# Attention probabilities of a fused kernel: both heads of a row tile side by side for all pairs, and six pairs instead of eight transposed in fp32 on TensorE

## The chip, the cores and the metric

The kernel runs on one core of a Trainium2 chip. The metric is the device time of one launch in microseconds (us), lower is better. Below, PE is TensorE (PEld its weight load), DVE is VectorE, ACT is ScalarE, POOL is GpSimd, and SP is the engine whose queue starts nearly all the DMAs.

## The reference

Three stages on a batch of 4, 448 tokens and 768 channels, all in fp32. First a causal attention with 12 heads of 64 channels; then a mixer over tokens and channels ("moe"); then a second mixer with sine and cosine ("moe2").

```python
scores = scale * np.matmul(q, k.transpose(0, 1, 3, 2))
mask = np.triu(np.ones((seq, seq), dtype=bool), k=1)
scores = np.where(mask, -1000000000.0, scores)
scores = scores - np.max(scores, axis=-1, keepdims=True)
attn = np.exp(scores)
attn = attn / (np.sum(attn, axis=-1, keepdims=True) + 1e-09)
return np.matmul(attn, v).astype(np.float32)
...
xt = x.transpose(0, 2, 1)
h = np.maximum(xt @ w_tok1, 0.0) @ w_tok2
u = x + h.transpose(0, 2, 1)
h2 = np.maximum(u @ w_ch1, 0.0) @ w_ch2
return (u + h2).astype(np.float32)
```

The second mixer follows on the result of the first and starts late in the kernel; the change does not touch it.

## The kernel before, in words

The heads are taken in 24 pairs, numbered 0 to 23, six to a batch element. A pair has seven score tiles (`TILES`): one shared tile for the first 64 rows of both heads (row tile 0, 128 columns), then for row tiles 1, 2 and 3 one tile for each head, 192, 320 and 448 columns wide. For a score tile, PE multiplies q with k into a PSUM bank (`ps_sc`, three banks), one DVE operation adds the mask and finds the row minimum of the negated scores while it writes them to SBUF (tile `sb`, line 367), and ACT takes the exponential with the row sum (line 369). The probabilities must then be transposed before PE can multiply them with v.

There are two ways for that. Pairs in `NATPV` (0 to 7) are *native*: PE transposes each 128-column block in fp32 into a PSUM bank (line 376), ACT copies the bank to SBUF (`pt`, line 378), and PE multiplies each block with v in fp32 (line 407), which the trace shows as two instructions for a product. The other pairs, 8 to 23, are *split*: the probabilities of both heads of a row tile stand side by side in one buffer (`both`); ACT makes an fp16 high part and DVE an fp16 low part of them (tile `ph`, lines 387 and 388; two buffers, one for row tiles 0 and 2, one for 1 and 3), one DMA on SP's queue transposes both parts (line 391), and PE makes three fp16 products for a block (lines 416 and 424). A split pair needs its v in two fp16 parts too (`value_squares`, `value_split`: one ACT pass, a small chain over PE, DVE and POOL, one POOL pass, one DVE pass at line 323). Native tiles rotate over three buffers for the probabilities and five for the transposed blocks.

Products with v are made four steps (score tiles) behind the scores for native pairs and five for split ones (`late_steps`). After each second pair comes the token mixing of these two pairs (`tokmix`: 24 short products with `xg`, then transposes and products with `wt2`). When the six pairs of a batch element are done, `split_ready` scales the result into fp16 tiles `ut`, and 72 units of 18 fp16 products with weights (`ch1_unit`, `ch2_unit`) follow, placed between the score tiles from step 53 (in pair 7) on by `UNIT_STEPS`. The weights arrive as float64 words and are rounded and split during the steps 14 to 92, on ACT, POOL and DVE (lines 177, 130, 185, 186, 163, 197), stored to DRAM and loaded again for each batch element.

Every engine works through its instructions in a fixed order that is settled when the kernel is built; score tiles and late steps have a raised priority in it. SP's queue is in order too, so that a DMA that waits for its source holds the loads and stores behind it.

Of the kernel before, what the change touches and what calls it, by code (L numbers as in the profile page):

```python
# [54 lines left out]
def fused(ctx, tc, q, k, v, w_tok1, w_tok2, w_ch1, w_ch2, w_theta, w_tok, w_ch, out):  # L55
# [198 lines left out]
    sb_all = ac.tile([P, BUFS["sb"] * 512], F32, tag="sb", name="sb")  # L254
    sbufs = [sb_all[:, j * 512:(j + 1) * 512] for j in range(BUFS["sb"])]
    for sb in sbufs:
        nc.gpsimd.memset(sb[:, 0:64], 0.0)
    pt_all = ac.tile([P, BUFS["pt"] * 512], F32, tag="pt", name="pt")
    ptfs = [pt_all[:, j * 512:(j + 1) * 512].rearrange("p (n q) -> p n q", q=P) for j in range(BUFS["pt"])]
    blocks = pt_all.bitcast(F16).rearrange("p (n q) -> p n q", q=P)  # L260
    count = [0]
# [135 lines left out]
    def pv(pp, i, h):  # L397
        if pp.ps is None:
            pp.ps = bank("pv", 1)
        reg = 0 if i == 0 else ((i - 1) * 2 + h + 2) * D  # L400
        if pp.native_pv:
            pt = pp.pts[i, h]
            blks = [8] if i == 0 else [6 + h] + [2 * u + h for u in range(i)]
            for u, vt in enumerate(blks):
                n = 2 * D if reg < 7 * D else D
# [6 lines left out]
        pt = pp.pts[i]
        reg = 0 if i == 0 else 2 * i * D
        if i == 0:
            for n, (blk, c) in enumerate(((0, 0), (0, 1), (1, 0))):
# [610 lines left out]
```

## Time and profile before

| | |
|---|---|
| median of 3 runs | 871.08 us (870.21 to 874.33) |
| profiled execution | 871.68 us, span on the core 869.9 us |
| PE busy | 839.3 us, 96% |
| DVE busy | 598.9 us, 69% |
| ACT busy | 531.3 us, 61% |
| POOL busy | 265.6 us, 31% |
| granted TensorE clock, mean | 0.998 |

The span runs from the first to the last instruction; 1.8 us of the device time lie around it. A busy PE here holds instructions that are pipelined, so that two can stand as busy at once, and a short wait can hide behind the end of the one before. What the shares hide is that the kernel has stages with different limits; they are read from windows below.

### The profile page before, as it was taken

To read this page: it belongs to the slowest core of one execution; us is meant where nothing else is said; L and a number is where in the kernel's file an instruction comes from. 1 tells how busy PE (TensorE), PEld (TensorE's weight loads), DVE (VectorE), ACT (ScalarE), POOL (GpSimd) and SP (SyncE) were. 2 spreads that over 40 slices of the span, in tenths; PEclk is the share of its full clock that TensorE was granted. 3 is DMA by queue.
4 is the path that set the end of the run, shared out by engine and by line. 5 is a ranking of instruction groups with operands and counts; after the bars stand their busy time and mean duration, and the time that the engine had idled before them with its cause. 6 is when DMAs were issued, how large, how long until landed. Compare 5 with 4: busy or idle time off the path is not lost.

```text
span 869.9 us, 16014 instructions
## 1 busy us (share of the span) xinstructions
PE 839.3 (96%) x5699; PEld 532.7 (61%) x5699; DVE 598.9 (69%) x1294; ACT 531.3 (61%) x1223; POOL 265.6 (31%) x445
## 2 busy tenths in 40 slices
PE   7999998899899999999999999999999999999997
PEld 6988856565657566576756655565555555555554
DVE  6788787999988556567774367669747548567541
ACT  6798786777767637367653276547647447456441
POOL 4366564547662220413222035331111001101000
PEclk9999999999999999999999999999999999999999
DMA  6866869999999976856475597702613123131012
GB/s 217 258 208 201 269 198 271 261 310 294 289 255 313 280 226 140 233 132 125 141 173 203 186 278 265 227 30 73 197 40 108 40 90 98 40 119 58 25 45 75
DMA packets 121024, 151.99 MB, mean 175 GB/s; under 512 B 76848, under 2 KB 88048, under 8 KB 120944
## 3 DMA queue, kind: packets, MB, share of 16 engines
q1 hardware_dynamic: 120400, 149.95, 59.4%
q0 software_dynamic: 384, 0.79, 0.4%
q8 instruction: 45, 0.74, 0.3%
q10 hardware_dynamic: 160, 0.23, 0.1%
q14 instruction: 35, 0.29, 0.1%
HBM read 110.56 MB, written 22.81 MB: 153 GB/s over the span
## 4 chain that ended last, share of the span: by engine, by line
PE 67%; DMA 10%; DVE 8%; ACT 5%; issue 5%; POOL 5%; SPq 0%; ACTq 0%; POOLq 0%; DVEq 0%
PE ps_mm L232 15%; PE ps_mm L231 15%; PE ps_mm L233 15%; DMA pt<-ph 5%; PE ps_sc L358 3%; PE ps_sc L231 3%; PE ps_sc L232 3%; PE ps_sc L233 3%; PE ps_pv L407 2%; DMA raw_w<-in_w_theta_dram 1%; PE ps_pv L424 1%; ACT junk L124 1%; ACT sb L369 1%; DVE sb L367 1%; PE ps_mm L376 1%
## 5 line engine op out<-in xcount | busy, mean ns | idle before, releaser
L231 PE MATMUL ps_mm<-h,ws 128*128 128x448 f16 x432 | 151.7, 354 | 1.6 <-DVE g L140 1.0
L232 PE MATMUL ps_mm<-h,ws 128*128 128x448 f16 x432 | 152.7, 354 | 0.1
L233 PE MATMUL ps_mm<-h,ws 128*128 128x448 f16 x432 | 152.5, 354 | 0.0
L231 PEld LDWEIGHTS <-ws 128*128 128x128 f16 x720 | 70.5, 98 | 67.2 <-issue 5.3
L233 PEld LDWEIGHTS <-ws 128*128 128x128 f16 x720 | 70.5, 98 | 63.9 <-issue 3.7
L232 PEld LDWEIGHTS <-ws 128*128 128x128 f16 x720 | 70.5, 98 | 62.5 <-issue 5.2
L369 ACT ACTIVATE sb<-sb,mx 128x320 f32<-128x320 f32 (+3 forms) x168 | 89.1, 533 | 25.6 <-DVE mx L367 25.0
L231 PE MATMUL ps_mm<-ut,ws 128*128 128x448 f16 x288 | 101.1, 353 | 1.4 <-DMA rawt<-x2d 1.3
L232 PE MATMUL ps_mm<-ut,ws 128*128 128x448 f16 x288 | 101.5, 353 | 0.8 <-DVE ut L197 0.8
L233 PE MATMUL ps_mm<-ut,ws 128*128 128x448 f16 x288 | 101.6, 353 | 0.0
L367 DVE CUSTOM_DVE_ANT_0 sb<-ps_sc,mask 128x320 f32<-128x320 f32 (+3 forms) x168 | 73.4, 455 | 17.7 <-PE ps_mm L376 11.3
L124 ACT ACTIVATE junk<-acc 128x448 bf16<-128x448 f32 x72 | 41.2, 572 | 59.1 <-DVE acc L912 41.3
L358 PE MATMUL ps_sc<-k_pad,q_raw 128*128 128x192 f32 (+3 forms) x168 | 56.9, 441 | 9.1 <-DMA k_pad<-in_k_dram 4.3
L787 POOL TENSOR_SCALAR tmp<-tmp 128x384 f32<-128x384 f32 x28 | 15.6, 556 | 148.6 <-ACT tmp L786 145.6
L388 DVE SCALAR_TENSOR_TENSOR ph<-sb,ph 128x128 f16<-128x128 f32 (+1 forms) x64 | 46.8, 736 | 19.0 <-ACT ph L160 18.3
L163 POOL TENSOR_SCALAR h<-t 128x448 f16<-128x448 f32 x48 | 35.2, 735 | 75.7 <-ACT t L497 75.2
L497 ACT ACTIVATE t<-ps_mm,c_scale 128x448 f32<-128x448 f32 x48 | 30.0, 625 | 41.3 <-PE ps_mm L233 36.2
L160 ACT ACTIVATE ph<-sb 128x128 f16<-128x128 f32 (+1 forms) x64 | 39.6, 625 | 25.6 <-DMA pt<-ph 25.3
L499 DVE TENSOR_TENSOR h<-t,h 128x448 f16<-128x448 f32 x48 | 32.0, 670 | 27.0 <-POOL h L163 26.9
L130 POOL TENSOR_SCALAR raw<-raw 128x768 f32<-128x768 f32 (+2 forms) x34 | 35.4, 1041 | 41.6 <-ACT wf L177 37.0
L231 PE MATMUL ps_sc<-th,ut 128*128 128x384 f16 x144 | 46.9, 326 | 0.0
L233 PE MATMUL ps_sc<-th,ut 128*128 128x384 f16 x144 | 46.8, 326 | 0.0
(218 smaller groups left out, 2119.4 us busy)
## 6 DMA issues: line engine op xcount, KB each, us to landing
ws<-w_c SPq DMA_DIRECT2D x120, 384.0 KB, 4.6
raw<-in_w_ch_dram SPq DMA_DIRECT2D x30, 768.0 KB, 5.6
w_c<-ws SPq DMA_DIRECT2D x30, 384.0 KB, 4.3
v_raw<-in_v_dram SPq DMA_DIRECT2D x24, 288.0 KB, 4.9
q_raw<-in_q_dram SPq DMA_DIRECT2D x12, 448.0 KB, 4.2
k_raw<-in_k_dram SPq DMA_DIRECT2D x12, 448.0 KB, 5.4
x2d<-acc SPq DMA_DIRECT2D x24, 224.0 KB, 3.8
acc<-x2d SPq DMA_DIRECT2D x24, 224.0 KB, 2.6
```

The lines of the kernel that those rows point to most:

```text
L124: nc.scalar.activation(j[:, 0:src.shape[-1]], src, AF.Square, accum_out=dst)
L130: nc.gpsimd.tensor_scalar(out=dst, in0=a, scalar1=b, scalar2=c, op0=ALU.mult, op1=ALU.mult)
L160: nc.scalar.activation(dst, src, AF.Copy, scale=scale)
L163: e.tensor_scalar(out=dst, in0=src, scalar1=scale, scalar2=0.0, op0=ALU.mult, op1=ALU.add)
L231: nc.tensor.matmul(ps, lhsT=ka(a[:, 0]), rhs=kb(b[:, 0]), start=first, stop=False)
L232: nc.tensor.matmul(ps, lhsT=ka(a[:, 0]), rhs=kb(b[:, 1]), start=False, stop=False)
L233: return nc.tensor.matmul(ps, lhsT=ka(a[:, 1]), rhs=kb(b[:, 0]), start=False, stop=last)
L358: nc.tensor.matmul(ps[:, 0:n], lhsT=lhs, rhs=cut(pp.kh), start=True, stop=pp.kl is None)
L367: pp.first = nc.vector.tensor_tensor_reduce(out=sb, in0=src, in1=msk, op0=ALU.add, op1=ALU.min, scale=-0.125, scalar=3.0e38, accum_out=pp. ...
L369: pp.last = nc.scalar.activation(sb, sb, AF.Exp, bias=pp.mx[:, j:j + 1], scale=-1.0, accum_out=pp.sm[:, 2 + j:3 + j])
L388: nc.vector.scalar_tensor_tensor(out=lo, in0=both, scalar=PSC, in1=hi, op0=ALU.mult, op1=ALU.subtract)
L499: gates[0] = nc.vector.tensor_tensor(out=t[:, 1], in0=f, in1=t[:, 0], op=ALU.subtract)
```

## The change

All pairs now lay the probabilities of both heads of a row tile side by side in `both`, native pairs too. A native row tile is transposed once both heads are there: 128, 384, 640 and 896 columns are 1, 3, 5 and 7 blocks, 16 for a pair, where 1, 2 x 2, 2 x 3 and 2 x 4 were 19 (the middle block now holds 64 columns of each head). Up to four blocks share a PSUM bank and an ACT copy, so that a pair has 6 copies and not 7. The number of fp32 products stays at 19. The three buffers for probabilities become two halves of the same memory, one for row tiles 0 and 2 and one for 1 and 3; the five buffers for transposed blocks become the fixed places that split pairs use. The products of both heads of a row tile are made in the step of the second head. Pairs 6 and 7 leave `NATPV` and become split pairs. The host's layout of k and v follows.

```diff
-BUFS = dict(ut=12, h2=8, acc=12, ws=8, wf=3, raw=3, sb=3, pt=5, t=3, junk=1)
+BUFS = dict(ut=12, h2=8, acc=12, ws=8, wf=3, raw=3, t=3, junk=1)
-NATPV = {0, 1, 2, 3, 4, 5, 6, 7}
+NATPV = {0, 1, 2, 3, 4, 5}
...
-        if pp.native_pv:
-            full = sbufs[count[0] % BUFS["sb"]]
-            sb = full[:, 64:64 + kk]
-        else:
-            both = (sb_all[:, 0:640], sb_all[:, 640:1536])[i % 2][:, 0:P if i == 0 else 2 * kk]
-            sb = both[:, h * kk:(h + 1) * kk]
+        both = (sb_all[:, 0:640], sb_all[:, 640:1536])[i % 2][:, 0:P if i == 0 else 2 * kk]
+        sb = both[:, h * kk:(h + 1) * kk]
...
-        if pp.native_pv:
-            nt = 1 + i
-            c0 = 64 if i == 0 else 0
-            pst = mm_bank()
-            for u in range(nt):
-                nc.tensor.transpose(pst[:, u * P:(u + 1) * P], full[:, c0 + u * P:c0 + (u + 1) * P], ident)
-            pt = ptfs[count[0] % BUFS["pt"]]
-            nc.scalar.activation(pt[:, 0:nt].rearrange("p n q -> p (n q)"), pst[:, 0:nt * P], AF.Copy)
-            pp.pts[i, h] = pt
-            count[0] += 1
-            return
         if i > 0 and h == 0:
             return
         m = both.shape[-1]
+        first = {3: 26, 2: 16, 1: (10, 0)[pp.pr % 2], 0: (8, 6)[pp.pr % 2]}[i]
+        if pp.native_pv:
+            pt = pp.pts[i] = blocks32[:, first // 2:first // 2 + m // P]
+            for u0 in range(0, m // P, 4):
+                pst = mm_bank()
+                nt = min(4, m // P - u0)
+                for u in range(nt):
+                    nc.tensor.transpose(pst[:, u * P:(u + 1) * P], both[:, (u0 + u) * P:(u0 + u + 1) * P], ident)
+                nc.scalar.activation(pt[:, u0:u0 + nt].rearrange("p n q -> p (n q)"), pst[:, 0:nt * P], AF.Copy)
+            return
```

The order moves at three places that matter below. In the rows, line numbers are those of each kernel; line 358 of before is line 349 of the changed kernel, 376 is 368, 407 is 400, 448 is 424, 367 is 354.

**First place.** PE, from the last score tile of pair 4 (448 columns) into pair 5 (its tile of 128 columns); `ident,sb` are transposes, `v_raw,pt` products with v, `xg` token mixing. Before:

```order
L358 MATMUL ps_sc<-k_pad,q_raw 128x448
L376 MATMUL ps_mm<-ident,sb 128x128 x2
L136 LDWEIGHTS ones
L136 MATMUL ps_mm<-tiny,ones 128x1
L376 MATMUL ps_mm<-ident,sb 128x128 x3
L407 MATMUL ps_pv<-v_raw,pt 128x128
L138 LDWEIGHTS ones
L138 MATMUL ps_mm<-sqb,ones 128x1
L358 MATMUL ps_sc<-k_pad,q_raw 128x128
L407 MATMUL ps_pv<-v_raw,pt 128x128 x2
L376 MATMUL ps_mm<-ident,sb 128x128 x3
L358 MATMUL ps_sc<-k_pad,q_raw 128x192
```

The changed kernel, from the same score tile:

```order
L349 MATMUL ps_sc<-k_pad,q_raw 128x448
L349 MATMUL ps_sc<-k_pad,q_raw 128x128
L368 MATMUL ps_mm<-ident,sb 128x128 x5
L400 MATMUL ps_pv<-v_raw,pt 128x128 x5
L349 MATMUL ps_sc<-k_pad,q_raw 128x192
L138 LDWEIGHTS ones
L138 MATMUL ps_mm<-sqb,ones 128x1
L424 MATMUL ps_mm<-xg_686,wt_184 128x256
L400 MATMUL ps_pv<-v_raw,pt 128x128
L424 MATMUL ps_mm<-xg_686,wt_184 128x256
L400 MATMUL ps_pv<-v_raw,pt 128x128 x4
L349 MATMUL ps_sc<-k_pad,q_raw 128x192
```

Before, the six transposes of pair 4's row tile 2 stand in two threes, one on either side of the tile that opens pair 5. Now its five stand together behind that tile. Those of row tile 3 (two fours before, seven now) come behind the token mixing that begins here, some forty rows further on, in both kernels.

**Second place.** PE, from the tile of 128 columns that opens pair 7. Before (the products are those of pair 6, in fp32):

```order
L358 MATMUL ps_sc<-k_pad,q_raw 128x128
L407 MATMUL ps_pv<-v_raw,pt 128x128 x5
L376 MATMUL ps_mm<-ident,sb 128x128 x3
L407 MATMUL ps_pv<-v_raw,pt 128x128 x3
L448 MATMUL ps_mm<-xg_1070,wt_184 128x256 x2
L358 MATMUL ps_sc<-k_pad,q_raw 128x192 x2
L457 MATMUL ps_mm<-ident_128,x_191 128x64
L459 MATMUL ps_mm<-ident,x_191 128x128 x3
L407 MATMUL ps_pv<-v_raw,pt 128x128 x3
L449 MATMUL ps_mm<-xg_1071,wt_184 128x256
L450 MATMUL ps_mm<-xg_1070,wt_184 128x256
L448 MATMUL ps_mm<-xg_1070,wt_184 128x256
```

The changed kernel, a little after the same tile:

```order
L349 MATMUL ps_sc<-k_pad,q_raw 128x192
L400 LDWEIGHTS pt
L400 MATMUL ps_pv<-v_hi,pt 128x128
L400 LDWEIGHTS pt
L400 MATMUL ps_pv<-v_raw,pt 128x128
L400 LDWEIGHTS pt
L400 MATMUL ps_pv<-v_hi,pt 128x128
L424 MATMUL ps_mm<-xg_1037,wt_184 128x256 x2
L400 LDWEIGHTS pt
L400 MATMUL ps_pv<-v_hi,pt 128x64
L400 LDWEIGHTS pt
```

The products of pair 6 are now fp16 products with `v_hi` and `v_raw` that read a block transposed by DMA, no transposes stand here, and the token mixing of pairs 4 and 5 (`xg`) comes behind the first of these products.

**Third place.** DVE, from the mask operation that opens pair 7 (`mask_181` is `mask0`, that of row tile 0). Before:

```order
L367 ISA sb,mx<-ps_sc,mask_181 128x128
L367 ISA mx 128x1
L127 TENSOR_SCALAR g<-g 128x1
L185 SCALAR_TENSOR_TENSOR wf<-wf,raw 128x768
L430 RECIPROCAL sm<-sm 128x7
L186 SCALAR_TENSOR_TENSOR wf<-raw,wf 128x768
L197 SCALAR_TENSOR_TENSOR ws<-wf,s,ws 128x768
L452 SCALAR_TENSOR_TENSOR h_1232<-ps_mm,h_1232 128x256 x2
L367 ISA sb,mx<-ps_sc,mask 128x192
L367 ISA mx 128x1
L467 TENSOR_TENSOR acc<-ps_mm,acc 128x448 x2
```

The changed kernel, from the same operation:

```order
L354 ISA sb,mx<-ps_sc,mask_181 128x128
L354 ISA mx 128x1
L374 SCALAR_TENSOR_TENSOR ph<-sb,ph 128x896
L185 SCALAR_TENSOR_TENSOR wf<-wf,raw 128x768
L354 ISA sb,mx<-ps_sc,mask 128x192
L354 ISA mx 128x1
L354 ISA sb,mx<-ps_sc,mask 128x192
L354 ISA mx 128x1
L197 SCALAR_TENSOR_TENSOR ws<-wf,s,ws 128x768
L374 SCALAR_TENSOR_TENSOR ph<-sb,ph 128x128
L186 SCALAR_TENSOR_TENSOR wf<-raw,wf 128x768
L428 SCALAR_TENSOR_TENSOR h_1229<-ps_mm,h_1229 128x256 x2
```

Between the mask operations of pair 7 there now stand the low parts (`ph`) of row tile 3 of pair 6 and of row tile 0 of pair 7, with the roundings (`wf`, `ws`) still among them.

## Rows read from the trace of the kernel before

**Rows 1.** Page: busy time and share of the span of each engine.

```profile
PE 839.3 (96%) x5699; PEld 532.7 (61%) x5699; DVE 598.9 (69%) x1294; ACT 531.3 (61%) x1223; POOL 265.6 (31%) x445
```

**Rows 2.** Windows: length, busy (count) per engine, PEclk, DMA share, GB/s.

```profile
5.12:79.66 74.54, 73.46 (x511) 63.72 (x511) 59.16 (x157) 61.94 (x176) 37.30 (x56) 1.00 0.74 231
79.66:130.09 50.43, 46.80 (x312) 35.61 (x311) 42.59 (x103) 40.45 (x105) 32.80 (x47) 1.00 0.73 224
113.85:130.09 16.24, 15.90 (x92) 10.07 (x93) 15.39 (x37) 12.69 (x33) 9.36 (x13) 1.00 0.59 152
130.09:148.72 18.63, 15.96 (x136) 12.19 (x135) 15.20 (x36) 10.98 (x30) 8.65 (x13) 1.00 1.07 269
148.72:305.50 156.78, 145.76 (x1200) 95.18 (x1197) 135.62 (x308) 111.18 (x269) 77.18 (x112) 0.99 1.04 284
305.50:869.90 564.40, 556.48 (x3543) 325.14 (x3543) 343.82 (x683) 305.47 (x647) 106.12 (x207) 1.00 0.44 130
```

**Rows 3.** DVE timeline (start, us): the mask operation that opens pairs 6 to 9.

```profile
79.66 0.28 DVE L367 CUSTOM_DVE_ANT_0 sb<-ps_sc,mask 128x128 f32<-128x128 f32 x1
...
91.53 0.28 DVE L367 CUSTOM_DVE_ANT_0 sb<-ps_sc,mask 128x128 f32<-128x128 f32 x1
...
113.85 0.28 DVE L367 CUSTOM_DVE_ANT_0 sb<-ps_sc,mask 128x128 f32<-128x128 f32 x1
...
130.09 0.28 DVE L367 CUSTOM_DVE_ANT_0 sb<-ps_sc,mask 128x128 f32<-128x128 f32 x1
```

**Rows 4.** Waits of DVE from 79 to 131: us in total, times, longest.

```profile
DVE ws L197 <- POOL ws L163: 3.4, 3, 1.8
DVE sb L367 <- PE ps_mm L376: 3.2, 3, 1.9
```

**Rows 5.** PE timeline: start, length, operation, count of merged instructions.

```profile
45.40 1.00 PE L407 MATMUL ps_pv<-v_raw,pt 128*128 128x64 f32 x8
46.24 0.97 PE L358 MATMUL ps_sc<-k_pad,q_raw 128*128 128x448 f32 x2
...
52.10 1.04 PE L376 MATMUL ps_mm<-ident,sb 128*128 128x128 f32 x8
52.97 0.17 PE L136 MATMUL ps_mm<-tiny,ones 128*128 128x1 bf16 x1
...
149.75 0.35 PE L233 MATMUL ps_mm<-ut,ws 128*128 128x448 f16 x1
149.94 0.35 PE L231 MATMUL ps_mm<-ut,ws 128*128 128x448 f16 x1
...
150.54 0.22 PE L424 MATMUL ps_pv<-v_hi,pt 128*128 128x64 f16 x2
150.60 0.19 PE L424 MATMUL ps_pv<-v_raw,pt 128*128 128x64 f16 x1
```

**Rows 6.** Page, costliest groups: busy us, mean ns; idle before, releaser.

```profile
L388 DVE SCALAR_TENSOR_TENSOR ph<-sb,ph 128x128 f16<-128x128 f32 (+1 forms) x64 | 46.8, 736 | 19.0 <-ACT ph L160 18.3
...
L160 ACT ACTIVATE ph<-sb 128x128 f16<-128x128 f32 (+1 forms) x64 | 39.6, 625 | 25.6 <-DMA pt<-ph 25.3
```

**Rows 7.** By tile (pt, then v_raw): duration ns min/median/max; DMA landing.

```profile
L391 SPq DMA_TRANSPOSE pt<-ph x64: 1172/1525/4723, 119.3 to 451.8; - x64
L378 ACT ACTIVATE pt<-ps_mm x56: 256/475/611, 9.6 to 116.2; 128x256 f32<-128x256 f32 x16, 128x384 f32<-128x384 f32 x16, 128x512 f32<-128x512 f32 x16, 128x128 f32<-128x128 f32 x8
...
DMA to landing us min/median/max: 2.3/4.3/9.1
...
L323 DVE SCALAR_TENSOR_TENSOR v_raw<-v_raw,sv,v_hi x16: 861/882/1512, 114.9 to 461.7; 128x576 f16<-128x576 f32 x16
```

**Rows 8.** Chain that ended last: start, us, what.

```profile
129.26 6.33 DMA pt<-ph
...
135.63 6.28 DMA pt<-ph
```

**Rows 9.** Tile sb to 130 us: idle of its engine until the release.

```profile
  PE ps_mm L376: 11.3, 13
```

More of the change, by code (lines that the diff above doesn't have):

```diff
@@ L252, in fused @@
     wt2 = ac.tile([P, 2, 2, S], F32R, tag="wt2", name="wt2")
[L254 to L261, printed above, removed]
+    sb_all = ac.tile([P, 1536], F32, tag="sb", name="sb")
+    pt_all = ac.tile([P, 2560], F32, tag="pt", name="pt")
+    blocks32 = pt_all.rearrange("p (n q) -> p n q", q=P)
+    blocks16 = pt_all.bitcast(F16).rearrange("p (n q) -> p n q", q=P)
     def tok_weights(n):
@@ L399, in pv @@
             pp.ps = bank("pv", 1)
[L400 to L405, printed above, removed]
-                rhs = twice(pp.v[0][:, vt * D:(vt + 1) * D]) if i == 0 else pp.v[0][:, vt * D:vt * D + n]
-                pp.pv = nc.tensor.matmul(pp.ps[:, reg:reg + n], lhsT=pt[:, u], rhs=rhs,
-                                 start=(u == 0), stop=(u == len(blks) - 1))
-            return
@@ L410, in pv @@
         if i > 0 and h == 0:
             return
[L412 to L415, printed above, removed]
-                pp.pv = nc.tensor.matmul(pp.ps[:, 0:2 * D], lhsT=pt[:, blk], rhs=twice(pp.v[c][:, 8 * D:9 * D]),
-                                         start=n == 0, stop=n == 2)
-            return
-        nb = 2 * i + 1
-        for h in range(2):
-            jobs = [(i, 6 + h)] + [(i + 1 + u if h else i - 1 - u, 2 * u + h) for u in range(i)]
-            for n, (blk, vt) in enumerate(jobs):
-                for m, (half, c) in enumerate(((0, 0), (0, 1), (1, 0))):
-                    pp.pv = nc.tensor.matmul(pp.ps[:, reg + h * D:reg + (h + 1) * D], lhsT=pt[:, half * nb + blk],
-                                             rhs=pp.v[c][:, vt * D:(vt + 1) * D], start=n + m == 0, stop=n == i and m == 2)
+        pt, nb = pp.pts[i], 2 * i + 1
@@ new lines, in pv @@
+        parts = ((0, 0),) if pp.native_pv else ((0, 0), (0, 1), (1, 0))
+        for h in range(2 if i > 0 else 1):
+            reg = (2 * i + h) * D
+            n = 2 * D if i == 0 or (pp.native_pv and reg < 7 * D) else D
+            if i == 0:
+                jobs = [(0, 8)]
+            else:
+                jobs = [(i, 6 + h)] + [(i + 1 + u if h else i - 1 - u, 2 * u + h) for u in range(i)]
+            for j, (blk, vt) in enumerate(jobs):
+                for m, (half, c) in enumerate(parts):
+                    v = pp.v[c]
+                    rhs = twice(v[:, vt * D:(vt + 1) * D]) if i == 0 else v[:, vt * D:vt * D + n]
+                    pp.pv = nc.tensor.matmul(pp.ps[:, reg:reg + n], lhsT=pt[:, half * nb + blk], rhs=rhs,
+                                             start=j + m == 0, stop=j == len(jobs) - 1 and m == len(parts) - 1)
@@ L962, in _lay @@
     rows = [slice(0, 64), slice(64, 192), slice(192, 320), slice(320, 448)]
-    native = np.array([n in NATPV for n in range(B * NPR)]).reshape(B, NPR, 1, 1)
     def pairs(a, tails_first):
@@ L970, in pairs @@
         else:
-            back = np.concatenate([t[..., 0, r] for r in rows[::-1]] + [t[..., 1, :]], axis=3)
-            t = np.where(native, t.reshape(B, NPR, D, 2 * S), back)
+            t = np.concatenate([t[..., 0, r] for r in rows[::-1]] + [t[..., 1, :]], axis=3)
         t = t.reshape(B, NPR, D, 2 * S)
@@ L982, in _lay @@
     zero = np.zeros_like(a0)
-    for x, y in ((a0, np.where(native, a0, zero)), (np.where(native, b0, zero), b0), (a0, b0)):
+    for x, y in ((a0, zero), (zero, b0), (a0, b0)):
         blocks.append(np.concatenate([x, y], axis=2))
```

20 lines of the change are left out of this document (7 added, 13 removed).

## The prediction

> **What bounds the kernel now.** I read the page first. PE is busy for 96% of the span and no other engine for more than 69% [rows 1], which looks like a kernel bound by PE from end to end. The windows correct that. Row tile 0 opens each pair, so its mask operation gives the start of a pair [rows 3], and I cut the span there [rows 2]. In pairs 0 to 5 (5.12 to 79.66) PE is busy 73.5 of 74.5 us: bound by PE. From 305.5 to the end it is busy 556.5 of 564.4 us: bound by PE too. In between it is not so plain. In pairs 6 to 8 (79.66 to 130.09) PE has 46.8 of 50.4 us and DVE 42.6; in pair 8 alone DVE has 15.39 of 16.24 us, 95%. In pair 9 both idle, with 16.0 and 15.2 of 18.6 us, and up to 305.5 PE is at 93% and DVE at 86%. Who is late in the split pairs is told by the chain that ended last: between 129 and 142 us it runs through two DMA transposes of 6.3 us each [rows 8]. So work taken from PE pays in pairs 0 to 5 and late, and work given to DVE costs in the middle.
>
> **Prices.** Eight transposes take from 52.10 to 52.97, so 0.109 us each; eight fp32 product instructions from 45.40 to 46.24, so 0.105, and a product is two of them, 0.21; fp16 products with v follow at 0.03 and a unit's products at 0.19 [rows 5]. A low part on DVE is 46.8 us / 64 = 0.73 us, a high part on ACT 0.62 [rows 6], an ACT copy of a bank 0.475 by its median, the low part of v 0.88 on DVE; a DMA transpose holds SP for 1.5 us and lands after 4.3, at most 9.1 [rows 7].
>
> **Pairs 0 to 5: side by side.** Three transposes less for a pair are 18 x 0.109 = 2.0 us of PE, in a stretch where PE is the bound, so they count. ACT loses one copy a pair, six in all, and DVE does the same work. What may be lost: two buffers in place of three. A mask operation must wait until the transposes of the tile whose buffer it takes are done; such waits cost DVE 11.3 us in 13 cases up to 130 us [rows 9], 0.87 each. At the first place of the order the tile of 192 columns in pair 5 (and in pair 3) waits behind seven transposes after the token mixing and no longer behind four: 3 x 0.109 = 0.33 us, twice, so 0.7. Elsewhere products, the next scores and token mixing stand between. I take -2.0 + 0.7 = **-1.3 us**; the bounds are -2.0 (no new wait) and +5.2 less 2.0, so +3.2 (one more such wait of 0.87 in each of the six pairs, all on PE's path).
>
> **Pairs 6 and 7: split.** PE loses 19 x 0.109 + 19 x 0.21 = 6.1 us a pair and gains 57 x 0.03 = 1.7 (and a few tiny matmuls for the scale of v): 4.4 less, 8.7 for both. ACT loses 14 copies of 0.475, 6.7 us, and gains eight high parts, 5.0 us, and two passes over v: about even. POOL gains two passes over v and is busy for 65% of the stretch (32.8 of 50.4 us), so I cost it at nothing; if that cover were gone, DVE's low part of v would wait for it. SP gains 8 x 1.5 = 12 us of issuing in 50; each transpose holds back what is queued behind it, which is a fetch of raw weights, a store of rounded ones or the v and k of the next pair. DVE gains 8 x 0.73 + 2 x 0.88 = 7.6 us. That is the point: in pairs 6 to 8 DVE's 42.6 become 50.2 us, about the whole 50.4 of the stretch, while PE's 46.8 fall to 38. The bound changes hands. DVE's idle time there falls, since two of its waits for PE go with the native tiles (3.2 us in 3 waits), but those for POOL's half of the weights (3.4 us) have no reason to go [rows 4]. I take the occupancy of pair 8, the only split pair in this stretch of before: 50.2 / 0.95 = 52.9 us, so **+2.5 us** against 50.4. Bounds: at 100% 50.2 us, -0.2; at the occupancy of pair 9, 15.2 / 18.63 = 82%, 61.5 us, +11. I stay near the dense end because the third place of the order shows the low parts set between masks and roundings, work that is ready at other times than they are.
>
> The 8.7 us of PE are thus spent on waiting, not on time. Some unit products move as well: 44 stand ahead of pair 9's first score before, 31 now (counted in the order); 13 x 0.19 are 2.5 us that PE must now do in pair 9, where it idles 2.7. Cost nothing, and 2.5 us if pair 9 becomes dense. From pair 10 on the same work stands in another mixture; I cost it at nothing and leave it to the range.
>
> **Sum.** 871.68 - 1.3 + 2.5 = 872.9 us for an execution like the profiled one, whose span is 869.9. That one lies 0.6 above the median of the three runs, so the forecast is **872.3 us**: no change that can be told. About 0.5%, 4.4 us, is what a measurement of this kernel can tell from none.
>
> **Two rules.** The trace says that in the middle neither engine alone sets the pace. The Trainium skill, "Perfetto Trace Analysis", section Identifying the Most-Contended Engine, says to improve the engine of highest occupancy first, and warns that the busy share of matmuls is no measure for TensorE. By its first half the 10.7 us of PE would all come off; by its second the 96% prove little. A second rule speaks against the change: "VectorE: DVE Perf Modes", section The three transpose paths, gives 390 ns for a 128x128 transpose of bf16 on TensorE and 1309 ns by DMA, and advises TensorE where PSUM will do. The rows agree in direction (0.109 us apiece on PE, 4.3 us to landing for a DMA of 2 to 14 blocks); what it would make of the time is the third rival.
>
> **Rivals.** *PE bound throughout* (0.12): all that PE loses counts, 2.0 + 8.7 = 10.7 us, 860.4 us. For it: 96% and the first and last stretch. Against it: DVE's 50.2 us cannot fit into 50.4 - 8.7 = 41.7.
>
> *The split stream settles earlier* (0.18): DVE runs pairs 6 to 8 without a gap (-0.2), pairs 0 to 5 give their 2.0, and pair 9, which idles now because pair 8 opened the stream of transposes in the midst of other work, finds it running and loses PE's idle 18.63 - 15.96 = 2.7. Together -4.9, 866.2 us. For it: pair 9 is bound by neither engine. Against it: PE's 2.5 us of units land in that very gap.
>
> *The transposes set the pace* (0.22), the other side: a pair uses each of its two `ph` buffers twice, and the next high part waits until the transpose before has landed; ACT stood 25.3 us for that [rows 6]. With landings of 5 to 6 us, between the median and the chain's [rows 7, 8] and 1.5 to 2 us for high part, low part and queues, four turns on two buffers are about 2 x 7.5 = 15 us. Pair 6 takes 11.9 us now. If it takes the 16.2 of pair 8, that is +4.3, and if pair 8 takes the 18.6 of pair 9 since its buffers are no longer free when it opens, +2.4 more; pair 7, 22.3 us long, covers its own. Less 1.3: +5.4, 876.5 us. It decides once transposes of pair 6 land later than some 4 us, so that two turns exceed 11.9.
>
> *Two buffers stall the native pairs* (0.06): +3.2 there and +2.5 behind, 876.8 us.
>
> **How the numbers follow.** No change has 0.42 by itself. Faster: 0.12 + 0.18 = 0.30. Slower: 0.22 + 0.06 = 0.28. The range must leave out at most two in ten: I drop the far end of the first rival and the far end of DVE's bound, and keep 863 to 881; the likeliest case alone would hold 868 to 876.
>
> **What would show it.** Side by side: pair 6 opens 1 to 2 us earlier than 79.66, with PE still busy at 98% before it. Split: DVE at 95% or more and PE near 75% between the openings of pairs 6 and 9, and that stretch 52 to 54 us long. If it is 42 to 47 us, the low parts were hidden and the first rival holds; if ACT's waits for transposes grow there and it is over 56 us, the third does. From 305 us on PE must be solid again, and the end follows the opening of pair 18 one for one. The prediction is wrong too if the mixture between pairs 10 and 17 moves by more than 4 us either way, which nothing in the rows decides, or if waits of PE drop the granted clock there: it is 0.99 or more in each window now.

## The result and the profile after

The changed kernel takes 877.33 us, median of 7 runs (874.17 to 879.67), against 871.08 for the kernel before (869.53 to 874.33): 1.007 of it, interval 1.0048 to 1.0093. That is 6.2 us slower, inside the stated range of 863 to 881; I had forecast 872.3 and put the largest weight, 0.42, on no change. The profiled execution spans 877.5 us (869.9 before); it took 879.3 us, 2.0 above the median.

First the windows of the changed kernel, cut at the openings of pairs as in [rows 2] (length, busy time and count of PE, PE's weight loads, DVE, ACT, POOL, then granted clock, DMA share, GB/s).

```profile
5.73:77.85 72.12, 70.15 (x479) 59.73 (x478) 56.44 (x153) 58.35 (x165) 37.12 (x53) 1.00 0.76 233
77.85:133.04 55.19, 43.51 (x337) 30.93 (x336) 47.03 (x115) 40.74 (x103) 36.65 (x54) 0.85 0.92 230
133.04:152.68 19.64, 16.72 (x127) 13.14 (x127) 17.29 (x39) 12.55 (x32) 10.05 (x15) 0.91 1.06 284
152.68:314.41 161.73, 147.69 (x1211) 95.82 (x1210) 139.14 (x310) 113.07 (x271) 76.33 (x111) 0.98 0.99 281
314.41:877.50 563.09, 556.19 (x3537) 324.68 (x3535) 341.22 (x682) 304.88 (x646) 105.75 (x206) 1.00 0.44 129
```

Read beside [rows 2]: pairs 0 to 5 are 2.4 us shorter, pairs 6 to 8 are 4.8 longer (55.19 for 50.43), pair 9 is 1.0 longer, pairs 10 to 17 are 4.9 longer (161.73 for 156.78), and the rest is 1.3 shorter. With 0.6 us of later start this is the 7.6 us between the spans. So the loss has two places of about equal size, and the second is one where the changed lines do nothing new. It is not quite the same work, though: DVE does 156.4 us in pairs 9 to 17, for 150.8 before, since some of what stood ahead of pair 6 or behind pair 18 now stands there (it does 2.7 us less ahead and 2.6 less behind).

PE's busy time fell by 4.2 us in all (page of the profile), not by 10.7:

```profile
PE 835.1 (95%) x5685; PEld 525.1 (60%) x5685; DVE 603.7 (69%) x1308; ACT 530.9 (60%) x1215; POOL 269.2 (31%) x448
```

Part of the reason shows at a finer cut, three microseconds each, within pairs 6 to 8 of the changed kernel:

```profile
84.00:87.00 3.00, 1.88 (x18) 1.88 (x18) 2.35 (x9) 3.00 (x9) 2.86 (x4) 1.00 0.55 152
87.00:90.00 3.00, 1.28 (x10) 1.05 (x7) 3.00 (x9) 2.19 (x6) 2.86 (x4) 0.89 0.49 101
90.00:93.00 3.00, 1.61 (x7) 0.86 (x5) 3.00 (x7) 1.67 (x4) 2.56 (x3) 0.50 1.06 311
93.00:96.00 3.00, 2.83 (x23) 2.84 (x24) 2.44 (x6) 2.77 (x6) 2.90 (x4) 0.50 1.30 311
96.00:99.00 3.00, 3.00 (x29) 2.75 (x29) 2.75 (x9) 2.95 (x11) 0.94 (x1) 0.97 1.43 259
...
105.00:108.00 3.00, 1.44 (x14) 0.99 (x13) 3.00 (x7) 1.93 (x6) 1.62 (x2) 1.00 0.99 288
108.00:111.00 3.00, 1.51 (x24) 1.09 (x24) 2.21 (x10) 2.91 (x9) 1.25 (x5) 0.81 1.05 191
111.00:114.00 3.00, 2.16 (x22) 1.50 (x18) 0.73 (x5) 3.00 (x8) 2.68 (x10) 0.50 0.96 282
114.00:117.00 3.00, 0.00 (x0) 0.00 (x0) 2.99 (x5) 3.00 (x8) 3.00 (x3) 0.50 1.01 386
117.00:120.00 3.00, 2.93 (x9) 1.21 (x10) 2.28 (x6) 1.23 (x4) 3.00 (x4) 0.50 1.32 344
120.00:123.00 3.00, 3.00 (x15) 1.60 (x14) 3.00 (x4) 1.37 (x5) 1.51 (x2) 0.99 1.06 92
```

From 84 to 90 PE works 3.2 us of 6 while DVE works 5.4; from 90 to 96 the granted clock is 0.50, the lower level of 1.2 GHz. The same comes again: from 105 to 111 PE works 3.0 us of 6, and from 111 to 120 the clock is 0.50. In the kernel before, the clock is 1.00 through this whole stretch [rows 2]. The Trainium skill, "TensorE: Matmul & The Clock Gate", Part 1, says that the gate knows two levels only, half and full; the windows at 0.50 and at 1.00 agree, and one between them, such as 0.81, can hold some of both. In the five windows at 0.50 PE is busy 9.5 us; at the full clock that would be about half, so some 4.8 of the 6.5 us that are missing are the clock's, by this estimate.

What is waited for in pairs 6 to 8: waits of ACT and then of DVE in the changed kernel from 77.85 to 133.04 (us in all, times, longest).

```profile
ACT ph L160 <- DMA pt<-ph: 8.4, 5, 3.5
...
DVE g L140 <- PE ps_mm L138: 3.2, 2, 3.0
DVE ph L374 <- ACT ph L160: 2.5, 2, 1.9
DVE ws L197 <- POOL ws L163: 1.2, 3, 0.7
...
DVE sb L354 <- PE ps_mm L368: 0.4, 1, 0.4
```

DVE's waits for POOL and for native transposes [rows 4] have shrunk from 6.6 to 1.6 us, and others stand in their place: DVE idles 8.2 us of this stretch, and 7.8 before. The chain that ended last in this stretch runs through landings of transposes (start, us, what):

```profile
87.13 0.90 DVE ph L374
88.09 5.03 DMA pt<-ph
93.20 0.96 ACT ph L160
...
95.33 7.50 DMA pt<-ph
102.90 0.53 ACT ph L160
103.46 0.56 DVE ph L374
...
106.73 3.99 DMA pt<-ph
```

It runs low part, transpose, next high part, transpose: the loop over the `ph` buffers of my third rival, 16.5 us of three landings. What this loop costs, the profile alone does not say.

Behind pair 9 three waits of PE have grown (changed kernel, 133.04 to 314.41; us, times, longest):

```profile
PE ps_sc L349 <- DVE mx L354: 6.3, 4, 4.1
PE ps_pv L400 <- DMA pt<-ph: 4.9, 5, 2.9
PE ps_mm L231 <- DMA ws<-w_c: 4.3, 3, 2.3
```

In the kernel before, from 130.09 to 305.5, they were:

```profile
PE ps_sc L358 <- DVE mx L367: 2.0, 3, 1.0
PE ps_pv L424 <- DMA pt<-ph: 1.1, 2, 0.8
PE ps_mm L231 <- DMA ws<-w_c: 0.6, 1, 0.6
```

Other waits of PE have shrunk there, so that its idle time grew by 3.3 us in all (17.0 for 13.7); the clock is 0.97 for 0.99. Why these waits grew, the profile does not say either.

### The profile page after: what moved, and what is told of

Its sections match the earlier page's. It is cut to its first block, busy times and chain, and to the rows that moved or that the text cites. A ratio compares the mean times of both kernels' runs of the same rounds, so it can differ in the third digit from the quotient of the medians.

```text
span 877.5 us, 15987 instructions
## 1 busy us (share of the span) xinstructions
PE 835.1 (95%) x5685; PEld 525.1 (60%) x5685; DVE 603.7 (69%) x1308; ACT 530.9 (60%) x1215; POOL 269.2 (31%) x448
## 4 chain that ended last, share of the span: by engine, by line
PE 71%; DMA 9%; DVE 9%; issue 4%; POOL 3%; ACT 3%; SPq 0%; DVEq 0%; ACTq 0%; POOLq 0%
PE ps_mm L231 17%; PE ps_mm L233 17%; PE ps_mm L232 16%; DMA pt<-ph 5%; PE ps_sc L349 4%; PE ps_pv L400 4%; PE ps_sc L231 3%; PE ps_sc L233 3%; PE ps_sc L232 3%; DVE sb L354 1%; DMA ws<-w_c 1%; DVE wf L185 1%; DVE ph L374 1%; DMA k_raw<-in_k_dram 1%; PE ps_mm L783 1%
## 5 line engine op out<-in xcount | busy, mean ns | idle before, releaser
L231 PE MATMUL ps_mm<-ut,ws 128*128 128x448 f16 x288 | 103.5, 362 | 7.1 <-ACT junk L124 3.9
L233 PE MATMUL ps_mm<-ut,ws 128*128 128x448 f16 x288 | 103.1, 358 | 0.0
L232 PE MATMUL ps_mm<-ut,ws 128*128 128x448 f16 x288 | 102.9, 357 | 0.0
L400 PE MATMUL ps_pv<-v_raw,pt 128*128 128x64 f16 (+3 forms) x570 | 66.1, 228 | 1.5 <-ACT pt L369 1.5
L374 DVE SCALAR_TENSOR_TENSOR ph<-sb,ph 128x128 f16<-128x128 f32 (+1 forms) x72 | 51.9, 727 | 20.8 <-ACT ph L160 20.4
L160 ACT ACTIVATE ph<-sb 128x128 f16<-128x128 f32 (+1 forms) x72 | 44.2, 622 | 23.6 <-DMA pt<-ph 23.4
L163 POOL TENSOR_SCALAR h<-t 128x448 f16<-128x448 f32 x48 | 32.3, 674 | 81.1 <-ACT t L473 80.6
L400 PE MATMUL ps_pv<-v_hi,pt 128*128 128x64 f16 (+1 forms) x684 | 40.5, 196 | 8.4 <-DMA pt<-ph 7.4
L400 PEld LDWEIGHTS <-pt 128*128 128x128 f16 x1026 | 37.1, 99 | 18.2 <-DMA pt<-ph 9.9
```

The costliest lines, as they stand in the source:

```text
L160: nc.scalar.activation(dst, src, AF.Copy, scale=scale)
L163: e.tensor_scalar(out=dst, in0=src, scalar1=scale, scalar2=0.0, op0=ALU.mult, op1=ALU.add)
L231: nc.tensor.matmul(ps, lhsT=ka(a[:, 0]), rhs=kb(b[:, 0]), start=first, stop=False)
L232: nc.tensor.matmul(ps, lhsT=ka(a[:, 0]), rhs=kb(b[:, 1]), start=False, stop=False)
L233: return nc.tensor.matmul(ps, lhsT=ka(a[:, 1]), rhs=kb(b[:, 0]), start=False, stop=last)
L374: nc.vector.scalar_tensor_tensor(out=lo, in0=both, scalar=PSC, in1=hi, op0=ALU.mult, op1=ALU.subtract)
```

## Experiments

Twelve kernels were run, each timed against the kernel before on the same chip (its median was 871.1 to 871.6 each time). One profiled execution of each is cut into the same stretches here; columns are the median time, then the length of pairs 0 to 5, 6 to 8, 9 to 17, of all behind the opening of pair 18, and DVE's busy time in pairs 9 to 17, all in us. A profile can lie some us off its median (the second layout kernel's does, by 5). A stretch can also be longer because work that stood elsewhere is done in it, since the order decides what stands on which side of a cut.

| kernel | time | 0 to 5 | 6 to 8 | 9 to 17 | from 18 | DVE, 9 to 17 |
|---|---|---|---|---|---|---|
| before | 871.1 | 74.5 | 50.4 | 175.4 | 564.4 | 150.8 |
| before, one element stored (same order) | 871.6 | 73.3 | 50.5 | 174.5 | 563.8 | 152.6 |
| before, one element stored (other order) | 881.5 | 73.3 | 50.5 | 186.7 | 562.7 | 151.0 |
| before, priority 250 | 875.1 | 73.1 | 50.4 | 175.8 | 570.8 | 150.2 |
| layout alone | 878.6 | 71.8 | 50.0 | 184.9 | 564.0 | 155.1 |
| layout alone, priority 250 | 880.2 | 72.0 | 49.9 | 183.2 | 563.1 | 155.8 |
| split alone | 878.9 | 76.7 | 52.5 | 173.9 | 569.7 | 150.3 |
| changed | 877.3 | 72.1 | 55.2 | 181.4 | 563.1 | 156.4 |
| changed, one element stored (same order) | 877.2 | 72.0 | 55.0 | 181.0 | 561.5 | 157.0 |
| changed, priority 250 | 878.8 | 71.8 | 55.1 | 179.9 | 565.6 | 155.8 |
| changed, units a step later | 879.7 | 71.8 | 54.5 | 177.3 | 568.1 | 157.2 |
| changed, units two steps later | 885.6 | 71.8 | 55.4 | 184.1 | 566.3 | 157.4 |
| changed, roundings earlier | 886.7 | 76.8 | 60.5 | 182.1 | 560.6 | 146.8 |
| changed, plain copies in pairs 6 and 7 | 885.2 | 71.9 | 52.7 | 187.1 | 566.0 | 156.2 |

**The layout alone.**

```
-NATPV = {0, 1, 2, 3, 4, 5}
+NATPV = {0, 1, 2, 3, 4, 5, 6, 7}      # in the changed kernel
```

> The changed kernel with pairs 6 and 7 native again: only the two heads side by side are left of the change. Theory A (the two added split pairs load DVE and the DMA engines in the middle, and that costs the time): the layout gives its 1.3 to 2.0 us and nothing is lost later, 868 to 871, against 871.1 before. Theory B (what the layout takes from PE moves the order that the scheduler writes for the pairs behind, and the middle comes out by chance of that order): anywhere between 866 and 878, with pair 9 opening 1 to 2 us earlier than 130.09 and the distance from pair 10 to pair 18 more than 3 us away from the 156.8 of before.

Measured 878.63 us, 1.0082 (1.006 to 1.0105). Theory A fails: with no split pair added, as much is lost as by the whole change. Of theory B the openings came (pairs 10 to 17 take 164.0 us for 156.8); the time lies 0.6 above its range. The windows (pairs 6 to 8, 9 to 17, the rest):

```profile
77.43:127.42 49.99, 44.69 (x289) 34.62 (x288) 40.03 (x101) 38.25 (x101) 30.56 (x46) 0.93 0.66 207
127.42:312.32 184.90, 167.09 (x1374) 110.21 (x1373) 155.12 (x347) 126.78 (x308) 88.73 (x128) 0.99 1.03 277
312.32:876.30 563.98, 555.39 (x3538) 324.40 (x3535) 340.63 (x680) 302.38 (x643) 104.24 (x206) 1.00 0.44 129
```

Pair 9 opens 2.7 us earlier than in the profile of before, and 1.8 earlier than in the other execution of that program below: where the layout is at work, it gives about what it promised. The loss lies between 127 and 312, in pairs whose code is that of the kernel before. (The buffers too: split pairs used the two halves of `sb` before as well.) What differs there is the order that the scheduler wrote, and with it what stands there: DVE does 4.3 us more in these pairs than before, though the kernel gives it nothing more to do. PE's scores wait for masks 5.7 us there, for 2.0 before.

**The split alone.**

```
-NATPV = {0, 1, 2, 3, 4, 5, 6, 7}
+NATPV = {0, 1, 2, 3, 4, 5}            # in the kernel before
-    count = [0]
+    count = [4]
```

> The kernel before with pairs 6 and 7 split, and the native pairs in their old layout (the ring of buffers for transposed tiles starts one further, since the last native tiles must not lie where pair 6 puts its first). Theory A: the whole loss is here, without the 1.3 us of the layout: 877 to 880. Theory B: pairs 6 to 8 take 53 to 56 us as in the changed kernel (55.2), but what follows between pair 10 and pair 18 differs from its 161.7 us by more than 3 either way, so that the time lies anywhere in 869 to 881. Theory C (the transposes set the pace of the split stretch): 877 to 880 too, with the loss between the openings of pairs 6 and 9.

Measured 878.94 us, 1.0072 (1.0045 to 1.0099), the time of theories A and C. But the stretches are longer in other places than theirs: 2.2 us in pairs 0 to 5, 2.0 in pairs 6 to 8, nothing in 9 to 17 (173.9), 5.3 behind pair 18. (Part of that is work that has moved: PE is busy 2.6 us more than before in pairs 0 to 5 and 2.2 more behind pair 18.) By theory B pairs 6 to 8 had to take 53 to 56 us, and they take 52.5; pairs 10 to 17, at 156.9, are as far from the change's 161.7 as it had them. Layout and split each cost 7 us and both together 6. Costs of work would add; these do not.

**A store of one element per partition, twice as a test of chance.**

```
-            pairs[b, pr] = Pair(b, pr, parts[b, pr])
+            pairs[b, pr], _ = Pair(b, pr, parts[b, pr]), nc.vector.memset(main.tile([P, 1], F32, tag='nil', name='nil'), 0.0) if b * NPR + pr == 6 else None
```

> The kernel before with one store of a single element per partition on DVE added at the first tile of pair 6, under 0.1 us of work and nobody waits for it; the scheduler nevertheless writes another order from there. Theory A: no change, 870 to 872, and the openings of pairs 9 to 18 within 2 us of before. Theory B: openings between pairs 10 and 18 move by 3 us or more and the end with them; a time 3 to 6 us away from 871.1, either way, is expected.

> The same added element in the changed kernel. Theory A: 876 to 879, the loss stays since its cause, the work of two more split pairs, is still there. Theory B: the time moves by 3 us or more away from 877.3, and as likely back to 871 as further away.

Measured 871.62 us (0.9995, 0.998 to 1.001) and 877.22 us (1.0061, 1.0038 to 1.0083). My expectation was wrong about the edit: counted afterwards, not one row of PE stands elsewhere, and DVE has the store and nothing else. So these two repeat the two programs. They show that the 6 us are steady from run to run, and that pairs 0 to 5 of the kernel before take 73.3 us in another execution, so that the 74.5 of its first profile lies a little high.

**The same store where pair 9 begins.** The source line is the same but for the number of the pair; the store itself stands early in DVE's order, yet behind the opening of pair 9 several hundred rows of PE and some 200 of DVE now stand elsewhere.

> The kernel before with one store of a single element per partition on DVE at the first tile of pair 9. At pair 6 the same element left the order as it was; here some 900 rows of PE stand in another order from pair 9 on, and 378 unit products stand ahead of pair 15 in place of 325, as in the kernel with the layout alone (368). The work is before's to within 0.1 us. If the order behind pair 9 is what the layout alone, the split alone and the change all lose on, this kernel loses too: 875 to 880, with 23 or more us for pair 14 and more than 20 us of PE idle between the openings of pairs 9 and 18 and DVE no busier than before in sum. If the loss belongs to what the edits do (fewer buffers, more split work), it stays at 870 to 873.

(The counts 378, 325 and 368 in that text were miscounted: 319 unit products stand ahead of pair 15 here, 306 before, 288 with the layout alone.) Measured 881.51 us, 1.0131 (1.0109 to 1.0152): **10 us lost with no work added**, more than the 875 to 880 expected. Pair 14 takes 29.5 us, as expected above 23; PE's idle time, 19.7 us, stays just short of the 20. Windows of this kernel, pairs 6 to 8, 9 to 17 and the rest:

```profile
79.06:129.54 50.48, 46.79 (x312) 35.61 (x311) 42.55 (x102) 40.55 (x105) 31.49 (x47) 1.00 0.74 226
129.54:316.22 186.68, 166.99 (x1341) 111.78 (x1340) 151.04 (x341) 123.81 (x299) 84.08 (x124) 0.96 0.99 265
316.22:878.90 562.68, 555.27 (x3538) 324.85 (x3536) 342.15 (x682) 304.49 (x646) 102.78 (x206) 1.00 0.44 130
```

and the second of them in the kernel before:

```profile
130.09:305.50 175.41, 161.72 (x1334) 107.37 (x1332) 150.82 (x341) 122.16 (x298) 85.83 (x124) 0.99 1.04 283
```

In pairs 6 to 8 the two agree to 0.1 us. Behind them DVE does the same 151 us of work and PE 1341 instructions for 1334, but the stretch is 11.3 us longer: 6.0 of them PE idle (19.7 for 13.7), 5.3 PE busy, at a granted clock of 0.96 for 0.99. Some 1.2 us of the latter are work that stood behind pair 18 before (555.3 for 556.5 us); the other 4 I put down to the clock, which is argued and not shown (a clock of 0.96 in 186.7 us leaves out 7.5 us, one of 0.99 in 175.4 us 1.8; so the size would fit). What PE waits for in it (us, times, longest):

```profile
PE ps_sc L358 <- DVE mx L367: 7.8, 7, 2.2
PE ps_pv L424 <- DMA pt<-ph: 2.5, 2, 1.8
```

In the kernel before these two were 2.0 and 1.1 us in that stretch. In all seven waits for a mask DVE works nearly without a break, 7.6 of the 7.8 us by the timeline: 3.1 us of it are masks, the rest other operations that stand ahead of the mask in the fixed order (`kl`, `ws`, `ut`, `qs` and more). So an order alone can do as much as the layout and the change did behind pair 9, with the same wait: 7.8 us here, 5.7 and 6.3 there. That it is the order that did it in those two is not shown by this, but nothing more than an order is needed.

**The same edit of the order on three kernels.**

```
-AHEAD, LAG, LOOK = 500, 4, 2
+AHEAD, LAG, LOOK = 250, 4, 2
```

> The kernel before with the priority halved from 500 to 250, as in the two runs with that edit on the layout alone (880.2) and on the changed kernel (878.8): 372 rows of PE in another order, from pair 13 on. If before's order is a favourable one and others are not, 873 to 878; if the work decides and not its order, 870 to 873.

> The kernel with only the layout (pairs 6 and 7 native), with the priority that lifts scores and their followers over the other work halved from 500 to 250: the same instructions, some 530 rows of PE in another order. The layout alone took 878.6 where its work is less than before's on PE, the same on DVE. If what it lost is the order that the scheduler happened to write (theory B), another order of the same work moves the time by 3 us or more, to 866 to 876. If the layout itself costs (two score buffers in place of three hold the later pairs), it stays within 2 us of 878.6.

> The same halved priority in the changed kernel: 446 rows of PE in another order. Theory B: away from 877.3 by 2 to 6 us, either way. Theory A (two more split pairs load DVE and the DMA engines, whatever the order): 876 to 879.

Measured: before 875.08 (1.0041, 1.0018 to 1.0064, its ten runs from 870.2 to 879.5), as its text had it if before's order is a favourable one; the layout alone 880.23 (1.009, 1.0065 to 1.0114) and the change 878.83 (1.008, 1.0064 to 1.0096), both within 2 us of where they were, which by the texts spoke for the work. It is no strong evidence: this edit leaves the order as it was up to pair 11 in the changed kernel and up to pair 13 in the other two, so only what follows was drawn anew. For the kernel before, the loss is all behind pair 18 (570.8 for 564.4 us, in a profile 2.4 us above the median), again with nothing added.

**Roundings earlier.**

```
-... [(14 + n * 78 // 23, n) for n in range(24)]
+... [(14 + n * 62 // 23, n) for n in range(24)]
```

> The changed kernel with the 24 roundings of weights spread over 62 steps in place of 78, so that they end in pair 10 and not in pair 13: six of their DVE operations go from the pairs behind 10 into pairs 2 to 9. If DVE's load in pairs 11 to 15 is what the change lost on (DVE there 0.89 to 0.99 busy), pairs 11 to 15 become 5 to 9 us shorter, pairs 6 to 9 2 to 4 us longer, and the time 870 to 875. If the pace there is set by the DMA engines (shares of 1.05 to 1.12) the fetches only move and the time stays at 876 to 879. By the third rival (transposes) it stays as well.

(The shares in that text are not those of the trace: in pairs 11 to 15 of the changed kernel DVE is busy 0.76 to 0.99, and the DMA share is 0.73 to 1.09.) Measured 886.65 us, 1.0172 (1.0154 to 1.0189): far above each of the expected ranges. Pairs 0 to 5 take 4.7 us more than in the changed kernel, and pairs 11 to 15 no less (112.4 for 111.2). Pairs 6 to 8 and 9 to 17:

```profile
82.63:143.16 60.53, 47.94 (x351) 33.73 (x349) 55.04 (x126) 45.52 (x114) 45.26 (x62) 0.83 0.96 257
143.16:325.26 182.10, 168.18 (x1335) 110.19 (x1336) 146.75 (x333) 120.73 (x294) 80.50 (x114) 0.96 0.95 259
```

In pairs 6 to 8, 8.0 us more of DVE go with a stretch that is 5.3 us longer. That fits a stretch whose pace DVE sets, and does not show it: a rounding runs on ACT, POOL and DVE, and POOL does 8.6 and ACT 4.8 us more there too. Behind pair 9, 9.7 us less of DVE (146.8 for 156.4) buy nothing: 182.1 us for 181.4. So the sum of DVE's work does not set the time there, in this order at least, which speaks against the last form of theory A, and against DVE's 5.6 us more in these pairs as the cause.

**Plain copies in place of the transposes of pairs 6 and 7.**

```
-NATPV = {0, 1, 2, 3, 4, 5}
+NATPV, PLAIN = {0, 1, 2, 3, 4, 5}, {6, 7}
...
-        pp.sent = nc.sync.dma_start_transpose(out=pt, in_=ph[:, 0:2 * m])
+        pp.sent = nc.sync.dma_start(out=pt.rearrange("p n q -> p (n q)"), in_=ph[:, 0:2 * m]) if pp.b * NPR + pp.pr in PLAIN else nc.sync.dma_start_transpose(out=pt, in_=ph[:, 0:2 * m])
```

> The changed kernel with the eight DMA transposes of pairs 6 and 7 replaced by plain DMA copies of the same bytes, so what the products of those two pairs read is not transposed; all else is as it was. If landings of transposes set the pace of pairs 6 to 8 (the third rival), that stretch falls from 55.2 to 50 us or less and ACT's waits for them there, 8.4 us in 5 cases, go. If DVE sets it (the forecast), the stretch stays at 53 to 55 us. For the end: 874 to 876 by the third rival if what is won there is kept, 876 to 879 by the forecast.

Measured 885.15 us, 1.0156 (1.014 to 1.0173), above both expected ranges. The order changes with this edit too, from pair 7 on: 20 unit products stand ahead of pair 9 in place of 31, for one thing. The stretch to pair 9, and ACT's waits in it:

```profile
77.59:130.29 52.70, 41.72 (x320) 29.93 (x319) 45.88 (x115) 40.68 (x104) 36.94 (x52) 0.90 0.83 246
...
ACT ph L160 <- DMA pt<-ph: 4.1, 3, 2.5
```

The stretch is 52.7 us where the change has 55.2, between the 50 and the 53 of the two expectations. The 2.5 us are no clean price of the transposes: 2.3 of them lie in pair 8 (21.7 for 24.0), whose order has changed and whose own transposes are still there, and 11 unit products fewer are some 2.1 us of PE's work. Pair 6 is the clean place, where DVE's order is the same in both. The changed kernel, this one, and the kernel before:

```profile
77.85:93.33 15.48, 10.75 (x72) 8.29 (x71) 13.85 (x39) 13.14 (x35) 13.35 (x18) 0.87 0.76 217
...
77.59:93.13 15.54, 10.74 (x82) 8.58 (x81) 13.77 (x39) 14.38 (x36) 13.41 (x18) 0.92 0.78 242
...
79.66:91.53 11.87, 10.79 (x77) 8.99 (x76) 11.04 (x27) 10.19 (x29) 8.06 (x11) 1.00 0.67 217
```

Pair 6 takes 15.5 us with transposes and with copies alike, though ACT waits 1.9 us for landings there with the one and 0.4 with the other. DVE is busy 13.9 of the 15.5 us, and none of its waits in it, 1.6 us in all, is for a high part or a landing. So in pair 6 the time goes with DVE's work, 2.8 us more than before, and not with the transposes. The Trainium skill, "VectorE: DVE Perf Modes", section Rules for kernel authors, advises TensorE for a 128x128 transpose where PSUM will do; the runs agree in direction, with 50.0 us in pairs 6 to 8 for the layout alone, which transposes pairs 6 and 7 on TensorE, and 55.2 with the change, but a split pair differs in more than its transposes.

**Units by another table.** Two tables chosen so that about as many unit products stand ahead of pairs 13 to 15 as in the kernel before.

```
-FIRST_UNIT, DENSE, RATE = 53, 88, (42, 29)
+FIRST_UNIT, DENSE, RATE = 53, 89, (41, 29)      # in the second kernel 53, 90, (40, 29)
```

> The changed kernel with the units released by another table: the 15th at step 89 in place of 88, and then 41 in 29 steps' spacing in place of 42. The work is the same. Counted in the order, 191, 252 and 316 unit products stand ahead of pairs 13, 14 and 15 (before 199, 252, 306; the changed kernel 213, 270, 326), and from pair 16 on the counts are within 11 of before's. If the change lost on the order that came out behind pair 12, an order nearer to before's gives 870 to 875, and the stretch from pair 12 to pair 16 falls from 91.5 us to 87 or less. If the two added split pairs cost it by their work, 876 to 880.

> The same with the 15th unit at step 90 and a spacing of 40 in 29: 198, 252 and 307 unit products ahead of pairs 13, 14 and 15, as before to within one, then 402 and 459 ahead of 16 and 17 (before 400, 432). By the order, 870 to 875, and the stretch from pair 12 to pair 16 87 us or less; by the work, 876 to 880. If both this kernel and the one with the table a step later stay at 877 or above, the number of units ahead of a pair is not what makes before's order good.

Measured 879.67 us (1.0106, 1.0084 to 1.0129) and 885.60 us (1.0166, 1.0142 to 1.019). Neither comes back. In the first, pairs 12 to 15 do take 84.0 us, under the 87 that were expected if the order decides, and pairs 9 to 17 177.3; it gives that back behind pair 18 (568.1). In the second they take 90.7, and the time is above both ranges. So the number of units ahead of a pair is not what makes before's order good. The two differ by 6 us with the same work.

## Why the prediction was off

The 877.3 us lie inside the range, and that is in part luck. The sum had +1.2 us; of the 7.6 us between the two profiles 6.0 came from pairs that it had cost at nothing. The range reached that far for other reasons, DVE's bound in pairs 6 to 8 and the third rival. Two rivals had nearly this time, the third with 876.5 and the one of two buffers with 876.8, and neither has its mechanism borne out below. Two of the prediction's own signs of being wrong came: pairs 10 to 17 moved by 4.9 us, where it allowed 4, and waits of PE dropped the clock, to 0.85 in pairs 6 to 8.

**Pairs 0 to 5, -1.3 us: right.** In the eight kernels of the table with the new layout and the old roundings they take 71.8 to 72.1 us, in the three kernels that share before's order there 73.1 to 73.3. That is 1.0 to 1.5 us (2.4 against the first profile of before). The mechanism shows too: PE is busy 69.3 to 70.2 us there, for 72.3 to 72.7, and idles 1.8 to 2.6, for 0.6 to 0.8, so that some of the saving goes into waits, as the sum had it. The rival in which two buffers stall the native pairs is out.

**Pairs 6 and 7 split, +2.5 us: right in direction, too small, and DVE not as dense.** PE fell behind DVE as forecast (79% busy for DVE's 85%) and the stretch is 55.2 us, not 52.9. The sign that was to show it, DVE at 95%, did not come, and neither did the third rival's, a stretch of over 56. It is 54.5 to 55.4 in all five kernels that split pairs 6 and 7 in the new layout with the old roundings and transposes. Two terms were off. DVE's work rose by 4.4 us, not 7.6. The groups of DVE's instructions there (count, then busy us, mean ns, idle before) in the changed kernel,

```profile
L374 DVE SCALAR_TENSOR_TENSOR ph<-sb,ph 128x128 f16<-128x128 f32 (+3 forms) x11 | 8.0, 731 | 2.5 <-ACT ph L160 2.5
...
L319 DVE SCALAR_TENSOR_TENSOR v_raw<-v_raw,sv,v_hi 128x576 f16<-128x576 f32 x3 | 2.6, 882 | 0.7 <-POOL v_hi L163 0.7
...
L167 DVE TENSOR_TENSOR xg<-x,xg 128x512 fp32r<-128x512 f32 x3 | 2.0, 676 | 0.0
```

and in the kernel before,

```profile
L167 DVE TENSOR_TENSOR xg<-x,xg 128x512 fp32r<-128x512 f32 x4 | 3.4, 851 | 0.0
...
L388 DVE SCALAR_TENSOR_TENSOR ph<-sb,ph 128x128 f16<-128x128 f32 (+2 forms) x3 | 3.0, 1000 | 0.0
...
L323 DVE SCALAR_TENSOR_TENSOR v_raw<-v_raw,sv,v_hi 128x576 f16<-128x576 f32 x1 | 0.9, 862 | 0.0
```

show the eight low parts at 5.0 us and the two of v at 1.7, 6.7 in all, near the price; but an operation of 1.4 us on `xg`, and one step of a rounding (7 and 6 of its two steps before, 6 and 6 after), moved out of the stretch. And the occupancy of 0.95, which I took from pair 8 alone, came out at 0.85: DVE's idle time, 7.8 us in [rows 2], stayed 8.2 where I let it fall to 2.7. The two errors work against each other: DVE's real 47.0 us at 0.95 would have been 49.5. The third rival seems to fit, with pair 6 at 15.5 us (16.2 forecast for it), but pair 6 takes the same with plain copies. Pair 8 takes 24.0 us (18.6 forecast), but work has moved into it from pair 7, which takes 15.7 us for 22.3; the two together take 39.7 for 38.6:

```profile
109.03:133.04 24.01, 19.20 (x146) 11.28 (x144) 20.21 (x47) 16.65 (x40) 16.21 (x27) 0.79 0.89 230
```

That is 146 instructions of PE and 47 of DVE, for 92 and 37 before [rows 2]. That the stretch with plain copies, 52.7 us, comes near my 52.9 confirms nothing either: DVE works 45.9 us in it and not 50.2. A higher clock did not shorten the stretch: in the second execution of the same order it was 0.88, for 0.85, and the stretch 55.0. And even these 4.8 us are not all work, since the split in the old layout has only 2.0 here.

**What PE saves: mostly spent, as said, but also on the clock.** Of 10.7 us PE's busy time fell by 4.2, and its idle time from the first pair to the end rose by 11.2 (26.3 to 37.5 by the windows). I had named the drop of the clock as a thing that would make the forecast wrong, and put no price on it. (In pair 10 it was 0.91 before already, which a window of eight pairs hid.)

**"From pair 10 on the same work stands in another mixture; I cost it at nothing": this step failed.** Pairs 9 to 17 are 6.0 us longer, 4.9 of them from pair 10 on, and PE's scores wait there for masks 6.3 us in place of 2.0. The kernel before runs on an order that is better than the two others tried: with the same work, these take 875.1 and 881.5. Every kernel here whose order differs from it lies between 875 and 887, whatever was edited. The 871 of before is thus in part a property of its order, and each edit here that made the scheduler write anew gave some of that up. I should have taken a loss as the likelier side of an unknown order, not zero. By stretches, the pairs that the change rewrites have -1.3 and +4.8 us, 3.5 in all. That the rest came with the order is argued: an order alone was shown to cost as much there in the kernel before, and no run gives the changed kernel a good one.

**The end.** PE is solid from pair 18 on (98.8% busy), and the 8.9 us of delay at its opening become 7.6 at the end: right within 1.3 us.

**What stays open.** Which of the swapped rows makes before's order good was not found; the count of units ahead of a pair is not it. Two of the three waits of PE that grew behind pair 9 are for DMA landings, 9.2 us for 1.7; in the second execution of the same program these are 4.9 (the wait for masks 6.1), and whether they follow from the order or from fuller DMA engines no run tells apart. And whether the change would win or lose over many orders cannot be told from these: its four (877.3, 878.8, 879.7, 885.6) and before's three (871.1, 875.1, 881.5) overlap. No kernel run here beats the kernel before.

## What to carry to other kernels

Where a scheduler writes the order, repeat the kernel before with the same work in another order (a lowered priority, a store of one element that does move rows) before a few us are put down to an edit: here that alone was worth 4 to 10 us. Price a stretch that turns to another engine by the idle time that this engine already has there, which stayed here (7.8 and 8.2 us), and not by its densest pair. Before a longer stretch is put down to a wait in it, look at what work the order has moved across its ends. And work taken from PE pays only where PE sets the pace: here 10.7 us of it were taken, PE's idle time grew by 11.2, and in the gaps the granted clock fell to 0.50.
